# A three-stage fp32 kernel on one core: stores of a feature tile one tile later, attention loads and weight sums at other steps

## The chip, the cores and the metric

One core of a Trainium2 chip runs the whole program. The metric is the device time of one execution in microseconds (us); the times below are medians of repeated runs. The kernel is straight-line code: every engine has its own in-order list of instructions, and the order in those lists is the order in which the Python code records them. The engines are called PE (matrix multiply), DVE, ACT and POOL (element-wise work), and SP, which here only issues DMA transfers.

## The reference

Pooled attention, then two feed-forward layers, all in float32 (weights come as 64-bit floats):

```python
# attention: q, k, v are (8, 8, 576, 64); k and v are averaged over groups of 8 positions
scores = scale * q @ k_p.T
attn = softmax(scores)
x = (attn @ v_p)            # -> (4608 tokens, 512)
# first layer, w_in 512x2048, w_out 2048x512
h = x @ w_in
x = (h * clip(h + 3, 0, 6) / 6) @ w_out
# second layer, w_gate and w_val 512x1536, w_out2 1536x512
g = x @ w_gate
y = (g * sigmoid(g) * (x @ w_val)) @ w_out2
```

## The kernel before

Tokens come in nine blocks of 512 (`NB` = 9, index `j`). The program has four parts, which follow each other on PE.

**Start-up.** Attention of block 0 alone: its loads, its scores, its exponentials, until the step `block_end[0]`.

**First stage**, blocks j = 0 to 8. For each of 16 feature tiles `f` (`F1` = 16, "a slot") PE makes one tile of `h` from 12 matmuls of 128x512 (`up`, L609; two halves of a float32 split make three matmuls for each of four depth pieces). Between two such groups of 12 the attention of block j + 1 is woven in: `steps` is a list of small steps, sorted by lags from the tables `when` and `when_startup`, and `attn_slot` records the next few of it. The letters are the kinds of step: P transposes queries (DVE, L471), S makes scores (PE, L489), X takes the maximum (DVE, L499, and a subtraction at L509), A the exponential (ACT), N and M normalise (DVE, then POOL at L537), E and F split the tail (ACT, then POOL or DVE at L552), T transposes (PE, L559 and L563), U, L and V multiply with the values (PE, L587 to L590), W and Y write `x` (ACT, DVE at L602). RK and K prepare a head's keys (POOL at L390, PE at L414), R0, R1 and R a head's values (POOL at L433: `v_in` and the tail `vts`), and Q makes the low half of the values (DVE, L453 and L455); Q is the last reader of the head's `v_in` and `vts`.

After each slot's matmuls comes `gate`: DVE makes the tile `g` of the slot before (`gate1`, L625) in one of four buffers `g32`, and the tile is stored to DRAM (`store_g`, L629, 256 KB). In blocks 0 to 7 the store stands on SP's queue right behind its own gate. In block 8 it stands on ACT's queue, one gate later (`late`). ACT makes `t` from each `h` (L620). `h` has three PSUM buffers.

**Weights for the later stages.** `prep_at` gives each of 26 units ("preps": 8 of `w_out`, 12 of `w_gate`/`w_val`, 6 of `w_out2`) nine steps at slots counted from block 1 (slot 16 x (j - 1) + f): 0 loads four quarters into two `stg` buffers of three (L121, 4 x 256 KB), 1 rescales (ACT, L133), 2 and 3 join two integer halves (DVE, L139 and L142) into `q`, 4 makes four sums in `q` (POOL for the first 20 units, L205 or L210; DVE for the other six), 5 and 6 copy to `s` (ACT, L266), 7 and 8 subtract (DVE, L269), and behind 8 the unit's 1792 KB are stored from `s` (SP, L273 or L278). `q` and `s` have one buffer each.

**Second and third stage.** 63 products of the first layer's second matrix (L873) by a seven-product scheme, with the six last units made beside them, and then the second layer (L694). Their loads start in block 8: `first_loads` names loads of `gq` (L832) and `pw` (L839), 1024 KB each, at slots 0 to 9, and eight more `pw` loads follow the last tile.

**Loads of the attention** are all on SP. They are not recorded where their buffer becomes free, but a number of steps later, by the list `later`: queries (`q_in`, L374) 12 steps behind P, keys (`k_in`, L306) 8 behind RK or K, the values (`vts`, L326, and `v_in`, L319 and L320) 8 behind Q. SP takes its list in order: a transfer that waits (for a buffer, for a result to store, or for the completion of the transfer eight places ahead of it, since eight completion counters are used in turn) holds up all behind it.

Of the kernel before, what the change touches and what calls it, by code (L numbers as in the profile page):

```python
# [23 lines left out]
def kernel(  # L24
# [27 lines left out]
    nc = tc.nc  # L52
    P = 128
    B, H, S, D = q.shape
# [5 lines left out]
    F1 = w_in.shape[1] // P  # L60
    F2 = w_gate.shape[1] // P
    N = 512
    NB = NT // N
# [40 lines left out]
    NP1 = F1 // 2  # L104
    g_d = [dram.tile([P, 2, 2, NP1, MB], F32, name=f"g{j}") for j in range(NB)]
# [110 lines left out]
    prep_t = {}  # L216
    prep_at = {}
    PREP_A = 20
    for u in range(len(preps)):
        first = 11 * u // 2 if u < PREP_A else F1 * (NB - 1) + 9 * (u - PREP_A)  # L220
        for step, off in enumerate((0, 3, 4, 5, 6, 7, 8, 8, 9)):
            prep_at.setdefault(first + off, []).append((u, step))

    def prep_slot(n):
# [4 lines left out]
    def prep_step(u, step):  # L229
        kind, f, m = preps[u]  # L230
        if step == 0:
            place = A7 if kind == "up" else B7
            prep_t["q", u] = []
            for pair in ((("11", "21"), ("12", "22")) if kind == "up" else (("11", "21"), ("22", "12"))):
                t = stg_p.tile([P, WC, 2], F32, tag="stg", name="wstg")
                for i, quarter in enumerate(pair):
                    r, c = int(quarter[0]) - 1, int(quarter[1]) - 1
                    if kind == "up":
                        w = (w_gate, w_val)[m].bitcast(I32).rearrange("(k p) f -> p k f", p=P)
                        src = w[:, 2 * c:2 * c + 2, 2 * P * (2 * f + r):2 * P * (2 * f + r + 1)]  # L240
                    else:
                        row = P * (2 * f + r if kind == "dn" else NP1 * r + f)
                        w = (w_out2 if kind == "dn" else w_out).bitcast(I32)[row:row + P, :]
                        src = w[:, 4 * P * c:4 * P * (c + 1)]
                    fetch_into(t[:, WH * i:WH * (i + 1)], src)
                a, b = (place[quarter] for quarter in pair)
                prep_t["q", u].append((t, slice(a, b + 1, b - a)))
        elif step == 1:
            for s, _ in prep_t["q", u]:
                rescale(s)  # L250
        elif step in (2, 3):
            if step == 2:
                prep_t["f", u] = q7_p.tile([P, 8, WH], F32, tag="q7", name="q7")
            s, at = prep_t["q", u].pop(0)
            join(s, prep_t["f", u][:, at].bitcast(I32), 2)
        elif step == 4:
            q, eng = prep_t["f", u], nc.gpsimd if u < PREP_A else nc.vector
            if kind == "up":
                sums_a(eng, lambda n: q[:, A7[n]])
            else:  # L260
                sums_b(eng, lambda n: q[:, B7[n]])
        elif step in (5, 6):
            if step == 5:
                prep_t["s", u] = s7_p.tile([P, 7, 2, WH], F32R, tag="s7", name="s7")
            q, t, part = prep_t["f", u], prep_t["s", u], slice(0, 4) if step == 5 else slice(4, 7)
            nc.scalar.copy(out=t[:, part, 0], in_=q[:, part])  # L266
        else:
            q, t, part = prep_t["f", u], prep_t["s", u], slice(0, 4) if step == 7 else slice(4, 7)
            nc.vector.tensor_tensor(out=t[:, part, 1], in0=q[:, part], in1=f32(t[:, part, 0]), op=ALU.subtract)  # L269
            if step == 7:  # L270
                return
            if kind == "up":
                nc.sync.dma_start(  # L273
                    out=s_up[f][m].rearrange("p s a k f -> p (s a k f)"),
                    in_=f32(t).rearrange("p s a f -> p (s a f)"),
                )
            else:
                nc.sync.dma_start(out=(s_dn if kind == "dn" else s_w1)[:, :, f], in_=f32(t))  # L278
# [344 lines left out]
    def gate1(t, ps):  # L623
        g = t_p.tile([P, N], F32, tag="g32", name="g32", bufs=4)
        nc.vector.scalar_tensor_tensor(out=g, in0=t, scalar=1.0, in1=ps, op0=ALU.min, op1=ALU.mult)  # L625
        return g

    def store_g(eng, j, f, g):
        eng.dma_start(out=g_d[j][:, :, f // NP1, f % NP1], in_=g.rearrange("p (r n) -> p r n", r=2))  # L629

# [285 lines left out]
    units, unit_end, segs, heads = [], [], [], []  # L918
    seg_of, first_in_seg, first_in_head = {}, {}, {}
    for j in range(NB):  # L920
        t0 = j * N
        while t0 < (j + 1) * N:
            b, s0 = t0 // S, t0 % S
            n = min(S - s0, (j + 1) * N - t0)
# [3 lines left out]
            for p in range(KT):  # L928
# [7 lines left out]
                s = s0  # L936
                for m, qt in alone:
                    u = (b, (p,), s, m, qt)
# [5 lines left out]
                if paired and p % 2 == 1:  # L944
                    u = (b, (p - 1, p), s, paired, paired)
# [26 lines left out]
    for i in range(NU):  # L972
        startup_unit = i < unit_end[0]
        lag = dict(when_startup if startup_unit else when)
        if units[i] in early_units and not startup_unit:
            lag["A"] = lag["X"]
        stages = [(what, i) for what in "SXANMEFTULVWY"]
        if 2 <= i < 8:
            stages.append(("C", i))
        stages += [("P", n) for n in first_in_seg.get(i, ())]  # L980
        for h in first_in_head.get(i, ()):
            stages += [(what, h) for what in ("RK", "K", "R0", "R1", "R", "Q")]
        events += [(i + lag[st[0]][0], lag[st[0]][1], st[1], n, st) for n, st in enumerate(stages)]
    steps = [e[4] for e in sorted(events, key=lambda e: e[:4])]
    block_end = [1 + steps.index(("Y", e - 1)) for e in unit_end]
    for what, i in steps[:block_end[0]]:
        if what == "S":
            block_end[0] = max(block_end[0], 1 + steps.index(("X", i)), 1 + steps.index(("A", i)))

# [61 lines left out]
    def next_v(i):  # L1053
        for load, ahead in ((load_vtail, 2), (load_v, 3)):
            for h in next_heads(i, ahead):
                later.append((done[0] + 8, lambda load=load, h=h: load(*heads[h], nc.sync)))

    def do_step(st):
        what, i = st
# [51 lines left out]
    done, later = [0], []  # L1111
# [10 lines left out]
    with tc.manual_schedule():  # L1122
# [6 lines left out]
            out=vmask[:, 0], in_=vmask[:, 0], compare_op=ALU.is_ge, fill=0.0,  # L1129
# [3 lines left out]
            out=vmask[:, 1], in_=vmask[:, 1], compare_op=ALU.is_ge, fill=0.0,  # L1133
# [41 lines left out]
        gated, late = [], []  # L1175

        def gate():
            for jd, fd, t, hp in gated:
                g = gate1(t, hp)
                for args in late:  # L1180
                    store_g(nc.scalar, *args)
                late.clear()
                if jd < NB - 1:
                    store_g(nc.sync, jd, fd, g)
                else:
                    late.append((jd, fd, g))
            gated.clear()

        first_loads = dict(enumerate([
# [28 lines left out]
                        split_b(0, f - F1 + NCB)  # L1218
        gate()
        for args in late:  # L1220
            store_g(nc.scalar, *args)
        new_pw(6, big_x("pw"))
        for n in (3, 4, 5, 6):
            for h in range(2):
# [8 lines left out]
        for i in range(7 * NB):  # L1233
            j, n = divmod(i, 7)
# [85 lines left out]
```

## Time and profile before

| | us |
|---|---|
| median of 3 runs (lowest, highest) | 1828.6 (1827.26, 1830.62) |
| the profiled execution | 1828.44 |
| its span, first to last instruction | 1826.7 |
| start-up and first stage, up to the last `h` | 648.7 |
| of it the five blocks 2 to 6 | 344.7 |
| second and third stage | 1178.0 |

The span is 1.7 us shorter than the execution's time. The blocks are cut where the first matmul of each block's `h` starts on PE; blocks 2 to 6 run from 205.2 to 549.9 us.

### The profile page before, as it was taken

How to read it: one execution, taken by the hardware profiler on the slowest of the kernel's cores; microseconds unless marked ns; L12 is line 12 of the kernel's file. 1: busy time of each engine (PE TensorE's matmuls, PEld its weight loads, DVE VectorE, ACT ScalarE, POOL GpSimd, SP SyncE). 2: the span in 40 equal slices, each digit the busy share in tenths (PEclk: the TensorE clock that was granted, in tenths of full speed). 3: DMA queues.
4: the chain of work that ended last, by engine and by line, in shares of the span. 5: the costliest groups of instructions: out<-in, count | busy, mean ns of one | idle time of the engine just before them, and what ended most of it. 6: DMA issues, size and time to landing. Idle time of an engine off the chain costs nothing.

```text
span 1826.7 us, 30898 instructions
## 1 busy us (share of the span) xinstructions
PE 1725.1 (94%) x11209; PEld 1624.9 (89%) x11209; DVE 1328.9 (73%) x2356; ACT 754.7 (41%) x1657; POOL 632.9 (35%) x812
## 2 busy tenths in 40 slices
PE   5789989988989989999999899999999999999999
PEld 4668777877768789999999799999999999999999
DVE  6587778887766358878888667667678568668666
ACT  5454545544535244545554323224224224124222
POOL 6245556756542000000000153153252351361550
PEclk8799999999989999999999899999999999999999
DMA  6556878877766885455544587887887977977876
GB/s 162 136 160 181 255 237 245 283 207 244 227 191 229 332 326 197 164 191 191 179 179 162 201 289 240 296 290 235 312 277 245 321 253 252 327 248 262 282 244 216
DMA packets 235831, 432.47 MB, mean 237 GB/s; under 512 B 86688, under 2 KB 168608, under 8 KB 218528
## 3 DMA queue, kind: packets, MB, share of 16 engines
q1 hardware_dynamic: 229184, 425.00, 70.7%
q10 hardware_dynamic: 6496, 5.51, 0.9%
q8 instruction: 88, 1.44, 0.3%
q14 instruction: 63, 0.52, 0.1%
HBM read 326.11 MB, written 104.33 MB: 236 GB/s over the span
## 4 chain that ended last, share of the span: by engine, by line
PE 72%; DMA 6%; DVE 4%; POOL 1%; SPq 1%; issue 1%; ACT 1%; ACTq 0%; DVEq 0%; POOLq 0%
PE b L694 43%; PE b L873 19%; PE h L609 8%; DMA g<-g 3%; DMA q_in<-in_q_dram 1%; PE pss L489 1%; DVE g L625 1%; DMA k_in<-in_k_dram 1%; DMA vts<-in_v_dram 1%; DMA y<-o 0%; SPq L374 0%; DVE s L269 0%; PE pst L563 0%; POOL k_in L390 0%; DVE q L142 0%
## 5 line engine op out<-in xcount | busy, mean ns | idle before, releaser
L694 PE MATMUL b<-xc,wr 128*128 128x384 f32 x3024 | 527.9, 335 | 9.0 <-ACT xc L147 5.0
L694 PEld LDWEIGHTS b<-xc,wr 128*128 128x128 f32 x3024 | 525.8, 188 | 9.9 <-ACT xc L147 5.3
L609 PE MATMUL h<-x,wu 128*128 128x512 f32 x1728 | 439.2, 406 | 6.1 <-DVE g L625 6.1
L741 POOL TENSOR_TENSOR s<-s,c 128x384 f32<-128x384 f32 x144 | 142.4, 1013 | 802.8 <-ACT s L739 802.8
L703 DVE TENSOR_TENSOR c<-c,b 128x384 f32<-128x384 f32 x504 | 265.1, 552 | 178.5 <-PE b L694 154.7
L609 PEld LDWEIGHTS h<-x,wu 128*128 128x128 f32 x1728 | 326.3, 194 | 73.5 <-DVE g L625 8.0
L873 PE MATMUL b<-gb,pw 128*128 128x256 f32 x3024 | 365.7, 284 | 7.5 <-ACT gb L147 5.9
L873 PEld LDWEIGHTS b<-gb,pw 128*128 128x128 f32 x3024 | 364.4, 192 | 8.8 <-ACT gb L147 6.3
L694 PE MATMUL b<-wr,gc 128*128 128x256 f32 x2268 | 265.6, 279 | 0.0
L694 PEld LDWEIGHTS b<-wr,gc 128*128 128x128 f32 x2268 | 265.4, 188 | 0.0
L147 ACT CAST gb<-gq 128x512 fp32r<-128x512 f32 x252 | 155.4, 622 | 179.8 <-PE b L873 154.5
L148 DVE TENSOR_TENSOR gb<-gq,gb 128x512 fp32r<-128x512 f32 x252 | 167.8, 687 | 63.0 <-ACT gb L147 62.3
L748 POOL TENSOR_TENSOR gf<-s,c 128x384 f32<-128x384 f32 x144 | 168.2, 1192 | 67.0 <-DVE c L703 64.5
L147 ACT CAST gc<-gf 128x768 fp32r<-128x768 f32 x126 | 105.6, 838 | 186.9 <-POOL gf L748 100.8
L739 ACT ACTIVATE s<-c 128x384 f32<-128x384 f32 x144 | 73.4, 526 | 204.0 <-DVE c L703 202.7
L148 DVE TENSOR_TENSOR gc<-gf,gc 128x768 fp32r<-128x768 f32 x126 | 133.7, 1092 | 15.7 <-ACT gc L147 14.0
L620 ACT ACTIVATE t<-h,half 128x512 f32<-128x512 f32 x144 | 98.9, 687 | 82.9 <-PE h L609 53.4
L625 DVE SCALAR_TENSOR_TENSOR g<-t,h 128x512 f32<-128x512 f32 x144 | 97.4, 677 | 38.9 <-DMA g<-g 26.6
L711 ACT COPY c<-b 128x384 f32<-128x384 f32 x72 | 33.9, 471 | 144.5 <-PE b L694 144.5
L851 DVE TENSOR_TENSOR gq<-gq 128x1024 f32<-128x1024 f32 x72 | 87.7, 1218 | 0.0
L537 POOL TENSOR_TENSOR e<-e,sm 128x288 f32<-128x288 f32 (+4 forms) x73 | 49.0, 671 | 106.5 <-DVE sm L533 81.2
L489 PE MATMUL pss<-kbd,qT 128*128 128x144 f32 (+2 forms) x320 | 60.5, 314 | 17.0 <-DVE qT L471 12.9
(106 smaller groups left out, 1669.8 us busy)
## 6 DMA issues: line engine op xcount, KB each, us to landing
wr<-sup SPq DMA_DIRECT2D x72, 1024.0 KB
wr<-sdn SPq DMA_DIRECT2D x84, 768.0 KB
wr<-sup SPq DMA_DIRECT2D x72, 768.0 KB
gq<-g SPq DMA_DIRECT2D x36, 1024.0 KB
g<-g SPq DMA_DIRECT2D x128, 256.0 KB
sup<-s SPq DMA_DIRECT2D x12, 1792.0 KB
wstg<-in_moe_w_out_dram SPq DMA_DIRECT2D x56, 256.0 KB
sw<-s SPq DMA_DIRECT2D x8, 1792.0 KB
```

Source lines behind the costliest of these rows:

```text
L147: nc.scalar.copy(out=hi, in_=src)
L148: lo_engine.tensor_tensor(out=lo, in0=src, in1=f32(hi), op=ALU.subtract)
L489: nc.tensor.matmul(out=ps[:, i], lhsT=qT[:, :qt], rhs=kbd_t[p], start=True, stop=True)
L609: nc.tensor.matmul(out=ps, lhsT=w(kt, wh), rhs=x(kt, xh), start=first and n == 0, stop=last and n == 3 * len(kts) - 1,)
L620: nc.scalar.activation(out=t, in_=ps, func=ACTF.Relu, bias=half, scale=1.0 / 6.0)
L625: nc.vector.scalar_tensor_tensor(out=g, in0=t, scalar=1.0, in1=ps, op0=ALU.min, op1=ALU.mult)
L694: nc.tensor.matmul(out=ps, lhsT=w(wh), rhs=x(xh), start=first and n == 0, stop=last and n == 2)
L703: add = lambda dst, a, b: nc.vector.tensor_tensor(out=dst, in0=a, in1=b, op=ALU.add)
L741: nc.gpsimd.tensor_tensor(out=g[q], in0=g[q], in1=c[q], op=ALU.mult)
L748: nc.gpsimd.tensor_tensor(out=gf[p][:, GP[TURN[q]], f], in0=g[q], in1=c[q], op=ALU.mult)
L851: nc.vector.tensor_tensor(out=v(what), in0=v(a), in1=v(b), op=op)
L873: nc.tensor.matmul(out=ps[:, d], lhsT=w[:, CB * c + k, wh, P * d:P * (d + 1)], rhs=g[:, gh, k], start=what == place and (c, d, k, m) == (0 ...
```

## The change

Five edits in one. `store_g` always goes to SP, and each tile's store is recorded ahead of the next tile's gate, in all nine blocks (`late`). The values' loads come 4 steps behind Q and no longer 8. For the units of block 1, S is followed at once by X and A (lag (1, 1) for both, S being at (1, 0)), where they had (1, 13); with it the loop that moved `block_end[0]` behind the X and A of every S that falls into the start-up is gone. The weight units that POOL sums start every 6 slots and no longer every 5.5, and have ten steps: sums two slots behind the second join, and the store in a step of its own, one slot behind the last subtraction.

```diff
-        first = 11 * u // 2 if u < PREP_A else F1 * (NB - 1) + 9 * (u - PREP_A)
-        for step, off in enumerate((0, 3, 4, 5, 6, 7, 8, 8, 9)):
+        first = 6 * u if u < PREP_A else F1 * (NB - 1) + 9 * (u - PREP_A)
+        for step, off in enumerate((0, 3, 4, 5, 7, 8, 9, 9, 10, 11)):
...
-        else:
+        elif step in (7, 8):
             q, t, part = prep_t["f", u], prep_t["s", u], slice(0, 4) if step == 7 else slice(4, 7)
             nc.vector.tensor_tensor(out=t[:, part, 1], in0=q[:, part], in1=f32(t[:, part, 0]), op=ALU.subtract)
-            if step == 7:
-                return
+        else:
+            t = prep_t["s", u]
             if kind == "up":
...
-    def store_g(eng, j, f, g):
-        eng.dma_start(out=g_d[j][:, :, f // NP1, f % NP1], in_=g.rearrange("p (r n) -> p r n", r=2))
+    def store_g(j, f, g):
+        nc.sync.dma_start(out=g_d[j][:, :, f // NP1, f % NP1], in_=g.rearrange("p (r n) -> p r n", r=2))
...
         if units[i] in early_units and not startup_unit:
-            lag["A"] = lag["X"]
+            lag["X"] = lag["A"] = (1, 1)
...
-    for what, i in steps[:block_end[0]]:
-        if what == "S":
-            block_end[0] = max(block_end[0], 1 + steps.index(("X", i)), 1 + steps.index(("A", i)))
...
-                later.append((done[0] + 8, lambda load=load, h=h: load(*heads[h], nc.sync)))
+                later.append((done[0] + 4, lambda load=load, h=h: load(*heads[h], nc.sync)))
...
             for jd, fd, t, hp in gated:
-                g = gate1(t, hp)
                 for args in late:
-                    store_g(nc.scalar, *args)
-                late.clear()
-                if jd < NB - 1:
-                    store_g(nc.sync, jd, fd, g)
-                else:
-                    late.append((jd, fd, g))
+                    store_g(*args)
+                late[:] = [(jd, fd, gate1(t, hp))]
             gated.clear()
```

SP's list in block 6, from one store to the loads of the last two heads' values. Before (`g_99` is the DRAM tile of block 6, the second name the buffer that is stored; each store also waits for DVE's gate of that very tile):

```order
325 L629 DMA g_99<-g_6128 256x1x256
326 L374 DMA q_in<-in_q_dram 32x16x32 x4
327 L121 DMA wstg<-in_moe_w_gate_dram 128x2x256 x4
328 L629 DMA g_99<-g_6193 256x1x256
329 L326 DMA vts_131<-in_v_dram 16x512 x3
330 L319 DMA v_in<-in_v_dram 72x512
331 L320 DMA v_in<-in_v_dram 56x512
332 L374 DMA q_in<-in_q_dram 32x16x32 x4
333 L629 DMA g_99<-g_6264 256x1x256
334 L326 DMA vts_132<-in_v_dram 16x512 x3
```

The same place of the changed kernel, on SP:

```order
321 L629 DMA g_99<-g_6032 256x1x256
322 L374 DMA q_in<-in_q_dram 32x16x32 x4
323 L326 DMA vts_131<-in_v_dram 16x512 x3
324 L319 DMA v_in<-in_v_dram 72x512
325 L320 DMA v_in<-in_v_dram 56x512
326 L629 DMA g_99<-g_6098 256x1x256
327 L273 DMA sup_108<-s_6007 128x3584
328 L374 DMA q_in<-in_q_dram 32x16x32 x4
329 L326 DMA vts_132<-in_v_dram 16x512 x3
330 L629 DMA g_99<-g_6163 256x1x256
```

The values' loads follow the queries at once; the store that stood between them is behind them, and stores a tile whose gate is a slot old. The weight loads are elsewhere.

SP's list in the start-up, before (`q_in` of 32x2x32 are the queries of the 64 tokens with which block 1 begins):

```order
20 L374 DMA q_in<-in_q_dram 32x2x32 x8
21 L121 DMA wstg<-in_moe_w_in_dram 128x4x256 x2
22 L306 DMA k_in<-in_k_dram 72x2x512
23 L374 DMA q_in<-in_q_dram 32x2x32 x8
24 L326 DMA vts_131<-in_v_dram 16x512 x3
25 L326 DMA vts_132<-in_v_dram 16x512 x3
26 L319 DMA v_in<-in_v_dram 72x512
27 L320 DMA v_in<-in_v_dram 56x512
```

And of the changed kernel, on SP at the same place:

```order
22 L306 DMA k_in<-in_k_dram 72x2x512
23 L326 DMA vts_131<-in_v_dram 16x512 x3
24 L326 DMA vts_132<-in_v_dram 16x512 x3
25 L319 DMA v_in<-in_v_dram 72x512
26 L320 DMA v_in<-in_v_dram 56x512
27 L319 DMA v_in<-in_v_dram 72x512
28 L320 DMA v_in<-in_v_dram 56x512
29 L319 DMA v_in<-in_v_dram 72x512
30 L320 DMA v_in<-in_v_dram 56x512
31 L374 DMA q_in<-in_q_dram 32x2x32 x8
```

The second eight query loads have moved behind twelve loads of values.

SP's list at the start of block 8 (`g_100` and `g_101` are the DRAM tiles of blocks 7 and 8). Before, where the stores of block 8 are on ACT's list:

```order
364 L629 DMA g_100<-g_7063 256x1x256
365 L832 DMA gq<-g_93 128x2048
366 L273 DMA sup_114<-s_7039 128x3584
367 L839 DMA pw<-sw_102 128x2048 x2
368 L832 DMA gq<-g_93 128x2048
369 L839 DMA pw<-sw_102 128x2048 x2
370 L832 DMA gq<-g_93 128x2048 x2
371 L839 DMA pw<-sw_102 128x2048 x10
```

The changed kernel, on SP:

```order
363 L273 DMA sup_112<-s_6980 128x3584
364 L839 DMA pw<-sw_102 128x2048
365 L629 DMA g_101<-g_7051 256x1x256
366 L121 DMA wstg<-in_moe_w_val_dram 128x2x256 x4
367 L839 DMA pw<-sw_102 128x2048
368 L629 DMA g_101<-g_7073 256x1x256
369 L832 DMA gq<-g_93 128x2048
370 L629 DMA g_101<-g_7098 256x1x256
371 L839 DMA pw<-sw_102 128x2048
372 L629 DMA g_101<-g_7123 256x1x256
```

The stores alternate with the large loads, and weight units 17 to 19 are not yet done: `sup_112`, and later `sup_113` and `sup_114`, are stored in block 8, where before it was `sup_114` alone, and one unit's four loads fall there too.

## Rows read from the trace of the kernel before

**Rows 1.** Windows by stage: stretch: length, busy PE, PEld, DVE, ACT, POOL (instructions), clock, DMA share, GB/s.

```profile
67.10:147.00 79.90, 71.17 (x402) 59.13 (x401) 59.98 (x133) 46.24 (x167) 38.16 (x62) 0.93 0.59 159
205.20:549.90 344.70, 308.00 (x1572) 255.82 (x1571) 266.02 (x623) 172.39 (x464) 210.76 (x326) 0.95 0.78 238
549.90:602.30 52.40, 52.40 (x265) 44.23 (x264) 35.71 (x76) 27.80 (x61) 12.60 (x20) 1.00 0.63 230
602.30:648.70 46.40, 44.42 (x194) 35.91 (x193) 14.35 (x20) 14.20 (x21) 0.00 (x0) 1.00 0.96 355
648.70:660.60 11.90, 6.59 (x50) 5.89 (x48) 3.80 (x6) 2.54 (x5) 0.00 (x0) 0.89 0.94 356
660.60:1020.00 359.40, 357.25 (x2962) 356.66 (x2963) 298.29 (x423) 180.36 (x297) 0.00 (x0) 0.99 0.53 186
1020.00:1826.70 806.70, 793.44 (x5307) 792.35 (x5306) 564.92 (x877) 249.57 (x422) 310.55 (x288) 0.99 0.79 269
```

**Rows 2.** Waits of the engines: us in total, times, longest us.

```profile
PE pst L563 <- POOL et L552: 30.0, 11, 8.4
POOL q L205 <- DVE q L142: 25.0, 6, 13.5
POOL vts L433 <- DMA vts<-in_v_dram: 24.1, 7, 8.4
```

**Rows 3.** Waits of SP's own queue, same columns, first row of the store's line.

```profile
SPq L629 <- DVE g L625: 48.2, 23, 9.7
```

**Rows 4.** Timeline of all engines around PE's longest stall: start, us, instruction [idle before <- what ended it].

```profile
509.22 0.52 SPq L629 DMA_DIRECT2D g<-g  x1
...
515.96 0.71 DVE L471 STREAM_TRANSPOSE qT<-q_in 128x512 f32<-128x512 f32 x1 [2.12 <-DMA q_in<-in_q_dram]
...
517.19 0.73 DVE L455 SCALAR_TENSOR_TENSOR vtl<-vts,vtl 32x64 fp32r<-32x64 f32 x1
...
519.34 0.52 SPq L629 DMA_DIRECT2D g<-g  x1
...
519.95 1.48 SPq L326 DMA_DIRECT2D vts<-in_v_dram  x3
...
524.97 1.64 POOL L433 TENSOR_TENSOR vts<-vts 96x256 f32<-96x256 f32 x3 [7.13 <-DMA vts<-in_v_dram]
...
528.98 0.34 PE L563 MATMUL pst<-ident,et 64*96 64x64 f32 x1 [8.36 <-POOL et L552]
```

**Rows 5.** Chain that ended last: twelve `h` matmuls behind two stalls, and undisturbed.

```profile
274.49 4.53 PE h L609 x12
...
529.31 5.42 PE h L609 x12
...
535.81 2.81 PE h L609 x12
```

**Rows 6.** Waits of the engines for stores of a tile.

```profile
DVE g L625 <- DMA g<-g: 26.6, 6, 5.8
...
ACT gb L147 <- DMA g<-g: 9.2, 1, 9.2
```

**Rows 7.** Timeline of all engines, start-up.

```profile
43.79 2.74 SPq L326 DMA_DIRECT2D vts<-in_v_dram  x6
...
45.23 0.24 DVE L471 STREAM_TRANSPOSE qT<-q_in 128x64 f32<-128x64 f32 x1 [0.61 <-DMA q_in<-in_q_dram]
...
45.82 0.69 DVE L142 SCALAR_TENSOR_TENSOR gb<-wstg,gb 128x512 int32<-128x512 int32 x1
...
49.55 6.53 SPq L374 DMA_DIRECT2D q_in<-in_q_dram  x8
...
57.96 1.33 PE L489 MATMUL pss<-kbd,qT 128*128 128x144 f32 x4 [6.63 <-DVE qT L471]
```

**Rows 8.** The page's DMA issues: how often, KB each.

```profile
sup<-s SPq DMA_DIRECT2D x12, 1792.0 KB
...
wstg<-in_moe_w_val_dram SPq DMA_DIRECT2D x24, 256.0 KB
```

More of the change, by code (lines that the diff above doesn't have):

```diff
@@ L1220 @@
         for args in late:
-            store_g(nc.scalar, *args)
+            store_g(*args)
         new_pw(6, big_x("pw"))
```

## The prediction

> **What bounds the kernel now.** I read the windows by stage first, because a change in one stage is worth what PE loses there, and not its share of the whole [rows 1]. The reader is to see two kinds of stretch. From 660.6 us to the end PE stands still for 359.40 - 357.25 = 2.2 us and 806.70 - 793.44 = 13.3 us: these stages are bound by PE's own matmuls, and since their PE list is the same in both kernels, I count nothing there. Blocks 2 to 6 are another matter: 344.70 us, of which PE works 308.00, so 36.7 us are stalls, at a mean granted clock of 0.95; and block 0 stalls for 79.90 - 71.17 = 8.7 us. Block 7 shows what a block is like without them: 52.40 us, no stall, clock 1.00.
>
> Next I ask what PE waits for there. The list of waits names the tail of the softmax: PE's transposes wait 30.0 us for POOL's `et` (L552), and POOL, just ahead of that instruction in its list, waits 24.1 us for the values' tails from DRAM and 25.0 us for DVE's joined weights [rows 2]. Then the timeline of the longest such stall, 8.36 us, read backwards [rows 4]: PE at 528.98 waits for POOL; POOL had waited 7.13 us, until 524.97, for a load of `vts` that SP issued only at 519.95. The buffer of that load was free when DVE's L455 (the step Q) ended, at 517.19 + 0.73 = 517.92. In between stood a store that waited for its own gate and was issued at 519.34. SP's own waits show that this is common: the store's line waits 48.2 us for the gate alone, 23 times, with further DVE instructions near it in rows behind [rows 3]. So the fault is one of order: SP holds loads back behind a result that is not there yet. After a stall PE also works at the lower of its two clock levels for a while: the 12 matmuls that take 2.81 us undisturbed take 4.53 us behind the first and 5.42 us behind the last of five stalls in blocks 2 to 6 [rows 5].
>
> **The change part by part**, against the profiled 1828.4 us (span 1826.7 and 1.7 around it; the median of the runs is 0.2 higher).
>
> *Blocks 1 to 6: stores one tile behind their gate, values 4 steps earlier, weight sums and weight stores a slot later.* A store now finds its gate done a slot ago, so SP's wait on it goes, and the 128 stores still cost the same 0.52 us of issue each. For the stall of 8.36 us: the load can follow Q directly, which is worth 519.95 - 517.92 = 2.0 us. Ahead of it in the same chain DVE sat 2.12 us waiting for queries, and their load too was issued behind a store, at 509.22; that wait can go as well. Together 4.1 of 8.36 us, one half. I found no second thing in the other stalls of this kind that would make them better or worse in proportion, so I take one half of all 36.7 us, 18 us. The wait of POOL for the joins (25.0 us) belongs to the same pool of stalls, since it delays the same `et`, and the sums that now stand a slot later remove it at the source; I don't add it a second time. The slow matmuls behind the five stalls cost some 10 us (1.7 and 2.6 us more behind the first and the last, 2 on the mean, five times); half of it, 5. **-23 us.** Bounds: nothing at all, if what comes next in the chain is as late (then SP waits for the landing of data instead), and -47, if all stalls go (36.7 + 10). A g32 buffer is held one slot longer: in blocks 0 to 7 DVE never waited for a store to land, all 26.6 us of that wait being in block 8 [rows 6], and four buffers with slots of some 4.3 us (344.70 / 80) leave three slots for a store, so I count zero; if it didn't fit, each miss would show as the 4 to 6 us that it takes in block 8.
>
> *Block 0: X and A straight behind S.* A score tile is given back to PE's ring of two as soon as ACT has made the exponentials, so key transposes that wait for it start earlier. The price is that DVE and ACT stand in order behind a score that PE has not made yet, ahead of `gate` and of L620. Of the 8.7 us I take a third, **-3 us**; bounds +3 and -8.
>
> *Start-up.* The values' loads, due 4 steps earlier, now stand ahead of the second eight query loads. Six of them take SP 2.74 us and the other six about as much, so the queries are issued some 5 us later, and DVE, which takes its list in order, makes their transposes not at 45.23 but at about 50.4 [rows 7]. Behind these stands the join that frees a weight buffer: it ended at 45.82 + 0.69 = 46.5 and will end at about 51.7. SP's next weight load waits for it, and behind that load stand the eight queries that were issued from 49.55 on and that the score waited for at 57.96, with PE idle for 6.63 us. SP came to them 49.55 - 46.5 = 3.0 us behind the join, part of it with the values' loads, so they slip by 5.2 less what of these 3.0 falls away: between 2 and 5 us. **+3 us**, bounds 0 (the transfers land sooner on a free queue) and +5. That `block_end[0]` is earlier moves one key transposition behind the first 12 matmuls; PE does both in either order, so nothing.
>
> *Block 8.* Two things. Six slots per unit instead of five and a half bring two more weight stores of 1792 KB and four weight loads of 256 KB into the block: 4.7 MB [rows 8], at the 355 GB/s of this stretch 13 us of transfers, in the only stretch of the first stage where the DMA engines are full (0.96 and 0.94 of their time) [rows 1]. And the 16 stores leave ACT's queue and stand between the large loads on SP. The Trainium skill speaks against that: Perfetto Trace Analysis, in its section DMA Optimizations, would give inputs and outputs to different issuing engines; by it alone this term would be the 13 us of its upper bound. In favour: ACT, whose first casts for the second stage stood 9.2 us behind its own stores [rows 6], is free, and PE's 11.90 - 6.59 = 5.3 us between the last `h` and the steady second stage fall into that wait. Transfers of slots 0 to 9 (10 loads of 1024 KB, the stores, three weight units) are more than ten slots of 2.8 us can carry, but slots 10 to 15 ask for little, so half of the 13 us should be caught up, and I count half of the 5.3 as gained: 6.7 - 2.7, **+4 us**, bounds -5 and +13.
>
> *Second and third stage.* The last six units get their later steps too, sums on DVE a slot later, the store a slot behind. PE never waited for them here; zero, with the same 15.5 us of stalls left as they are.
>
> Sum: 1828.4 + 3 - 3 - 23 + 4 = 1809.4, by the median 1809.6 us.
>
> **The rivals.** *Everything goes* (0.08): if the late issue is the only cause, all of blocks 2 to 6 is gained and most of block 0: -47 - 6 + 3 + 0, 1778 us. Against it: POOL's chain behind a landed `vts` is itself 4 us long (524.97 to 528.98), and DVE works 266.02 of 344.70 us, so it would be at 0.89 of the time if 47 us went.
>
> *The wait moves* (0.15): SP runs ahead of DVE, and stands a little later at the next thing, the Q step that the values' loads now wait for themselves, or the landing of the transfer eight places ahead. What the stores no longer wait, the loads do; the DMA engines are at 0.78 in these blocks, and `q_in` is issued in small pieces. Then -7 there, 0 in block 0, and the +3 and +4 stay: 1828.6 us, no change.
>
> *Block 8 decides* (0.16), on the other side: a store behind up to seven transfers of 1 MB on one queue lands after 7.3 MB / 355 GB/s, 20 us; DVE has four tile buffers and PE three of `h`, together some 10 us of slots, so gate, and with it PE, run at the pace of the transfers, and the whole 13 us fall on the path. With the start-up's 3 that is +16, and it decides where blocks 0 to 6 give back less than 16 us; with half of my gain there (-11) the time is 1833 us. The rule of the Trainium skill just cited would send it this way. For it speaks that the DMA share is 0.96 already, against it that PE lost just 46.40 - 44.42 = 2.0 us inside the block while stores took their time on ACT's queue.
>
> **How the numbers follow.** My forecast, one half of the stalls, has 0.61, and its own range is 1794 to 1824 (a quarter to three quarters of the blocks' 47, with the other terms at the sum). A measurement of this kernel tells a change from none at about 0.2%, 3.7 us. Faster: all of the forecast and of *everything goes*, and a fifth of *the wait moves*: 0.72. The same: 0.09, most of *the wait moves*. Slower: *block 8 decides* and a fifth of *the wait moves*, 0.19. For eight times in ten the range reaches from 1788, which leaves out *everything goes*, to 1834, which takes in both other rivals; the corner of all bad bounds (5 + 3 + 0 + 13, 1849) is left out.
>
> **What would show it.** In the profile after: SP's waits on the store's line fall from dozens of us to a few; loads of `vts` follow L455 within 1 us; POOL's waits for `vts` and for joins halve; the five stalls of PE in blocks 2 to 6 are shorter and the stretch takes about 320 us; the score at 57.96 comes at about 61; block 8 takes about 4 us longer up to the steady second stage. It is wrong if POOL still waits as long for `vts` though they were issued early, if DVE's gate waits for stores in blocks 0 to 7, or if block 8 lasts 10 us longer than 46.4.

## The result and the profile after

The changed kernel takes 1798.75 us (median of 4 runs, 1796.84 to 1801.43), the kernel before on the same chip 1829.3: a ratio of 0.9835, 95% interval 0.9818 to 0.9852, some 30 us less. The profiled execution took 1801.43 us, its span is 1799.6.

The windows by stage of the changed kernel, with the columns of [rows 1] and cut at the same places of the program (the first `h` matmul of a block; the last three rows divide the second and third stage elsewhere):

```profile
64.30:144.70 80.40, 72.40 (x433) 59.97 (x433) 62.94 (x136) 46.66 (x164) 41.81 (x67) 0.95 0.65 173
201.90:521.10 319.20, 302.56 (x1572) 251.11 (x1571) 267.17 (x614) 168.93 (x461) 205.47 (x318) 0.98 0.78 238
521.10:573.50 52.40, 52.40 (x265) 44.20 (x264) 33.83 (x74) 26.36 (x58) 12.67 (x20) 1.00 0.67 233
573.50:627.30 53.80, 48.01 (x195) 37.51 (x194) 22.63 (x33) 18.85 (x28) 5.74 (x8) 0.94 1.02 397
627.30:660.00 32.70, 29.59 (x243) 29.19 (x243) 20.23 (x28) 15.24 (x26) 0.00 (x0) 0.99 0.89 351
660.00:1000.00 340.00, 335.77 (x2789) 335.07 (x2787) 286.89 (x407) 171.72 (x281) 0.00 (x0) 1.00 0.52 183
1000.00:1799.60 799.60, 790.98 (x5286) 790.37 (x5286) 559.96 (x872) 246.07 (x417) 310.81 (x288) 0.99 0.79 268
```

25.5 of the 27.1 us by which the span is shorter are in blocks 2 to 6: 319.20 us where there were 344.70. PE does the same 1572 matmuls there; it is idle for 319.20 - 302.56 = 16.6 us instead of 36.7, and its busy time falls from 308.00 to 302.56 us, at a mean granted clock of 0.98 instead of 0.95. Block 8 is the one that got longer: 53.80 us instead of 46.40, its clock 0.94 instead of 1.00, idle 5.8 us instead of 2.0.

The waits of the engines in blocks 2 to 6 (201.9 to 521.1 us), which answer to [rows 2]:

```profile
PE pst L563 <- POOL et L552: 11.7, 4, 5.3
DVE qT L471 <- DMA q_in<-in_q_dram: 7.6, 6, 3.2
POOL vts L433 <- DMA vts<-in_v_dram: 7.3, 2, 5.2
POOL q L205 <- DVE q L142: 1.7, 1, 1.7
```

The same four rows of the kernel before, in its blocks 2 to 6 (205.2 to 549.9 us):

```profile
PE pst L563 <- POOL et L552: 28.8, 8, 8.4
POOL vts L433 <- DMA vts<-in_v_dram: 23.8, 6, 8.4
DVE qT L471 <- DMA q_in<-in_q_dram: 16.6, 6, 6.8
POOL q L205 <- DVE q L142: 9.6, 4, 4.7
```

All four fell: the transposes wait less for the softmax's tail, and what stood ahead of it in the chain (the queries, the values' tails, the joined weights) is late less often. The place of the stall of [rows 4], 8.36 us (the 143rd of 160 `et` transposes on PE in each kernel), reads in the timeline of the changed kernel:

```profile
490.46 3.92 SPq L326 DMA_DIRECT2D vts<-in_v_dram  x3
...
492.44 0.71 DVE L471 STREAM_TRANSPOSE qT<-q_in 128x512 f32<-128x512 f32 x1
...
496.44 2.00 POOL L433 TENSOR_TENSOR vts<-vts 96x256 f32<-96x256 f32 x3
...
501.25 0.26 PE L563 MATMUL pst<-ident,et 64*96 64x64 f32 x1 [1.65 <-POOL et L552]
```

The queries cost DVE no wait, POOL takes the values' tails without one, and PE stands still for 1.65 us.

### The profile page after: what moved, and what is told of

The parts are those of the page before. It is cut to its first block, busy times and chain, and to the rows that moved or that the text cites. A ratio compares the mean times of both kernels' runs of the same rounds, so it can differ in the third digit from the quotient of the medians.

```text
span 1799.6 us, 30919 instructions
## 1 busy us (share of the span) xinstructions
PE 1717.7 (95%) x11209; PEld 1618.0 (90%) x11209; DVE 1336.2 (74%) x2356; ACT 754.4 (42%) x1657; POOL 634.7 (35%) x812
## 4 chain that ended last, share of the span: by engine, by line
PE 69%; DMA 8%; DVE 4%; issue 1%; SPq 1%; ACT 1%; POOL 1%; ACTq 0%; DVEq 0%; POOLq 0%
PE b L694 44%; PE b L873 17%; PE h L609 7%; DMA pw<-sw 1%; DMA wstg<-in_moe_w_out_dram 1%; DMA g<-g 1%; DVE g L625 1%; DMA gq<-g 1%; DMA wstg<-in_moe_w_val_dram 1%; DVE s L269 1%; DMA y<-o 1%; DMA q_in<-in_q_dram 0%; PE pss L489 0%; SPq L374 0%; DMA vts<-in_v_dram 0%
## 5 line engine op out<-in xcount | busy, mean ns | idle before, releaser
L873 PE MATMUL b<-gb,pw 128*128 128x256 f32 x3024 | 364.2, 283 | 3.4 <-ACT gb L147 2.8
L873 PEld LDWEIGHTS b<-gb,pw 128*128 128x128 f32 x3024 | 363.6, 192 | 4.1 <-ACT gb L147 3.0
L625 DVE SCALAR_TENSOR_TENSOR g<-t,h 128x512 f32<-128x512 f32 x144 | 97.5, 677 | 33.5 <-DMA g<-g 23.5
L537 POOL TENSOR_TENSOR e<-e,sm 128x288 f32<-128x288 f32 (+4 forms) x73 | 47.4, 649 | 110.1 <-DVE sm L533 85.5
```

Of the source, the lines that this page charges most:

```text
L873: nc.tensor.matmul(out=ps[:, d], lhsT=w[:, CB * c + k, wh, P * d:P * (d + 1)], rhs=g[:, gh, k], start=what == place and (c, d, k, m) == (0 ...
```

## The experiments

The sum of the prediction laid the gain to the stores and the values' loads together. Against this stand two other readings: that another of the four parts makes it (weight units, start-up), or that no part does by itself, since what SP no longer waits for at one entry of its list it waits for at the next. Eight kernels take one part each, or all but one. All lengths in this table are in us, cut as above; the last column runs from the first `h` of block 8 to the end of the span. Ratios are to the kernel before on the same chip, with 95% intervals.

| kernel | median | ratio | start-up | block 0 | block 1 | blocks 2-6 | block 8 | from block 8 on |
|---|---|---|---|---|---|---|---|---|
| before | 1829.3 | 1 | 67.2 | 79.8 | 58.2 | 344.7 | 46.5 | 1224.4 |
| after | 1798.75 | 0.9835 (0.9818, 0.9852) | 64.3 | 80.4 | 57.2 | 319.2 | 53.7 | 1226.1 |
| stores_alone | 1824.28 | 0.9965 (0.9949, 0.9981) | 68.5 | 80.2 | 58.7 | 343.9 | 50.4 | 1223.8 |
| values_alone | 1831.72 | 1.0004 (0.9992, 1.0015) | 70.8 | 79.3 | 61.0 | 341.8 | 47.7 | 1226.7 |
| weights_alone | 1831.74 | 1.0009 (0.9997, 1.0021) | 66.7 | 79.1 | 57.2 | 345.9 | 54.5 | 1227.3 |
| early_alone | 1828.97 | 0.9983 (0.9970, 0.9996) | 61.8 | 83.8 | 58.7 | 345.9 | 47.4 | 1224.3 |
| after_old_stores | 1826.23 | 0.9977 (0.9965, 0.9988) | 63.7 | 81.1 | 57.2 | 342.7 | 55.0 | 1227.9 |
| after_old_values | 1799.25 | 0.9833 (0.9811, 0.9855) | 62.4 | 79.5 | 57.2 | 318.9 | 53.2 | 1225.8 |
| after_old_weights | 1813.93 | 0.9913 (0.9893, 0.9932) | 63.4 | 79.7 | 58.6 | 338.9 | 46.2 | 1222.7 |
| after_old_early | 1803.49 | 0.9847 (0.9827, 0.9867) | 69.0 | 79.2 | 57.2 | 318.1 | 53.3 | 1225.9 |

Block 7 takes 52.4 or 52.5 us in all of them. Kernels with the same start-up list differ there by about 1 us (63.2 to 64.3 over seven kernels), so less than that is not read. The lengths are those of one profiled execution: that of `stores_alone` took 1829.48 us, the longest of its eleven runs and 5.2 above the median, that of `after_old_weights` 1817.71, 3.8 above it, that of the changed kernel 2.7 above it.

**One part on the kernel before.** `stores_alone` stores one tile behind the gate, with block 8 still on ACT's queue:

```diff
                 for args in late:
-                    store_g(nc.scalar, *args)
+                    store_g(nc.scalar if args[0] == NB - 1 else nc.sync, *args)
...
+                late[:] = [(jd, fd, gate1(t, hp))]
```

> The kernel before, with the stores of blocks 0 to 7 one tile behind their gate on SP; block 8 keeps its stores on ACT, the rest is as before. If the order of SP's queue made the gain (the theory), this is the larger half of it: 10 to 16 us faster (1813 to 1819), blocks 2 to 6 some 12 us shorter than 344.7. If the weight units made it, or the place of the values' loads alone, it is within 4 us of the kernel before.

`values_alone` has the loads 4 steps behind Q:

```diff
-                later.append((done[0] + 8, lambda load=load, h=h: load(*heads[h], nc.sync)))
+                later.append((done[0] + 4, lambda load=load, h=h: load(*heads[h], nc.sync)))
```

> The kernel before, with the loads of the values 4 steps behind Q. Theory: 4 to 8 us faster (1821 to 1825), since the loads still stand behind stores that wait for their own gate. If the place of these loads alone made the gain: 15 to 25 us faster (1804 to 1814). If the weight units made it: no change.

`weights_alone` has the ten steps and the 6 slots (the change's first two pieces):

```diff
-        first = 11 * u // 2 if u < PREP_A else F1 * (NB - 1) + 9 * (u - PREP_A)
-        for step, off in enumerate((0, 3, 4, 5, 6, 7, 8, 8, 9)):
+        first = 6 * u if u < PREP_A else F1 * (NB - 1) + 9 * (u - PREP_A)
+        for step, off in enumerate((0, 3, 4, 5, 7, 8, 9, 9, 10, 11)):
...
```

> The kernel before, with weight units every 6 slots, ten steps, sums two slots behind the join and the store in a step of its own. Theory: 2 to 6 us faster in blocks 2 to 6, of which block 8 takes some back: within 4 us of the kernel before. If the weight units made the gain: 15 to 25 us faster (1804 to 1814).

`early_alone` has X and A straight behind S, and no loop that moves the end of the start-up:

```diff
-            lag["A"] = lag["X"]
+            lag["X"] = lag["A"] = (1, 1)
...
-    for what, i in steps[:block_end[0]]:
-        if what == "S":
-            block_end[0] = max(block_end[0], 1 + steps.index(("X", i)), 1 + steps.index(("A", i)))
```

> The kernel before, with X and A straight behind S for the units of block 1, and the start-up ending with its own last step. Theory: 1 to 5 us faster (1824 to 1828), from the stall of 2.59 us ahead of the first tile and the stalls of block 0; blocks 2 to 6 unchanged at 344 us. A rival by which the values' loads, and not this edit, made the start-up shorter has no change here.

No part alone gives more than 0.35%, and blocks 2 to 6 stay between 341.8 and 345.9 us in all four. The theory missed twice: `stores_alone` gained 6 us by the medians and not 10 to 16, `values_alone` nothing and not 4 to 8. `weights_alone` stayed within 4 us as it said, but gained nothing in blocks 2 to 6 where it said 2 to 6; `early_alone` is 1.5 us faster, inside its 1 to 5. The parts don't add: 0.35% and 0.17% are gained by the stores and by the start-up's edit, nothing by the other two, against 1.65% by all of them.

**All parts but one.** Each takes one of these pieces back from the changed kernel (in `after_old_stores` the stores of block 8 are again on ACT's queue).

> The changed kernel with the stores as before (blocks 0 to 7: on SP right behind their own gate; block 8: on ACT). No part alone shortened blocks 2 to 6 by more than 3 us, the change does by 25, so parts must need each other. Theory now: several things hold each late load back one after the other (store, distance from Q, weight units ahead of it), and each alone only uncovers the next; then taking any one out loses most: here 1812 to 1822, blocks 2 to 6 at 332 to 342. Rival, two parts make it (values and weights, say) and the stores are idle: 1797 to 1804, blocks 2 to 6 at about 320.

> The changed kernel with the values' loads 8 steps behind Q as before. Theory of several covers: loses most, 1812 to 1822. If stores and weight units are the pair that makes it: 1797 to 1804. POOL's wait for vts in blocks 2 to 6 (7 us after, 24 before) tells it beside the time.

> The changed kernel with the weight units as before (every 5.5 slots, nine steps). Theory of several covers: loses most, 1812 to 1822, although block 8 has less to move (its part is 7 us shorter). If stores and values are the pair: 1792 to 1802.

> The changed kernel with X and A of block 1's units at (1, 13) and the start-up that ends behind them, as before. They touch only the start-up and block 0, so by either theory 2 to 5 us are lost (1801 to 1804), all of it before 150 us, and blocks 2 to 6 stay at about 320. If the place at which the start-up ends decides what stands where in the later blocks: more than 8 us are lost, in blocks 2 to 6.

Two parts turn out to be necessary: without the late stores blocks 2 to 6 take 342.7 us, without the new weight units 338.9 (what `after_old_weights` keeps of the gain, 11 us of the span, is 5.8 us in these blocks, 3.9 in start-up and block 0, 1.7 from block 8 on). The values' 4 steps change nothing (318.9 us, total as after). The start-up's edit gives up to 4.7 us of the total by the medians, with overlapping intervals, and by the lengths 3.5 us in start-up and block 0. So the theory of several covers, by which any part taken out loses most, is wrong for the values' loads, and `after_old_stores` lost more than it said (1826.23 us for 1812 to 1822); the rival that stores and values are the pair is wrong by `after_old_weights`. Stores and weight units alone, without both other parts, were not run.

Why the stores alone bring little is seen in the waits of SP's own queue in blocks 2 to 6. Before:

```profile
SPq L629 <- DVE g L625: 31.1, 13, 9.7
SPq L629 <- DVE x L602: 17.4, 15, 2.7
...
SPq L273 <- DVE s L269: 6.1, 6, 2.5
...
SPq L278 <- DVE s L269: 4.0, 4, 2.9
```

`stores_alone`:

```profile
SPq L273 <- DVE s L269: 36.4, 7, 9.9
SPq L278 <- DVE s L269: 8.6, 6, 3.1
...
SPq L629 <- DVE g L625: 3.8, 8, 1.2
```

`after_old_weights`:

```profile
SPq L273 <- DVE s L269: 35.7, 8, 9.5
SPq L278 <- DVE s L269: 5.9, 3, 3.2
...
SPq L629 <- DVE g L625: 2.8, 7, 0.6
```

The changed kernel:

```profile
SPq L629 <- DVE aT L579: 19.2, 13, 3.9
SPq L629 <- DVE sm L531: 8.2, 6, 2.7
...
SPq L273 <- DVE s L269: 3.8, 3, 2.4
SPq L629 <- DVE g L625: 3.6, 5, 1.8
...
SPq L278 <- DVE s L269: 2.7, 2, 2.4
```

With late stores and the old weight units the wait for the gate is gone (31.1 us to 3.8 and 2.8), and a wait of the same size stands at the weight unit's store, which follows its own last subtraction: 6.1 + 4.0 us before, 36.4 + 8.6 in `stores_alone`, 35.7 + 5.9 in `after_old_weights`. With late stores and the new weight units, neither is there. The other way round, with the new weight units and the old stores, it is the store's line that waits: all its rows in blocks 2 to 6 sum to 81.3 us before, 97.5 in `weights_alone`, 93.6 in `after_old_stores` and 56.4 in the changed kernel. The stall of [rows 4] shows the same in the timeline of `after_old_weights`:

```profile
490.29 0.52 SPq L629 DMA_DIRECT2D g<-g  x1
...
498.28 0.94 DVE L269 TENSOR_TENSOR s<-q,s 128x768 fp32r<-128x768 f32 x1
...
499.29 0.35 SPq L273 DMA_DIRECT2D sup<-s  x1
...
500.26 4.89 SPq L374 DMA_DIRECT2D q_in<-in_q_dram  x4
...
508.25 0.71 DVE L471 STREAM_TRANSPOSE qT<-q_in 128x512 f32<-128x512 f32 x1 [2.20 <-DMA q_in<-in_q_dram]
...
510.61 1.33 SPq L326 DMA_DIRECT2D vts<-in_v_dram  x3
...
516.05 1.64 POOL L433 TENSOR_TENSOR vts<-vts 96x256 f32<-96x256 f32 x3 [5.99 <-DMA vts<-in_v_dram]
...
520.05 0.34 PE L563 MATMUL pst<-ident,et 64*96 64x64 f32 x1 [7.36 <-POOL et L552]
```

SP issues nothing from 490.81 to 499.29, until the subtraction that ends at 498.28 + 0.94 = 499.22; a store and a lot of queries follow, whose four issues take 4.89 us and for which DVE waits; behind them SP has another store, another lot of queries and four weight loads; the values' tails are issued at 510.61, POOL waits 5.99 us, and PE 7.36.

**Which piece of the weight units.** Two kernels divide them: `units_55` keeps the weight store in its own step and takes the rest back, `store_at_sub` keeps the 6 slots alone.

```diff
--- units_55, against the changed kernel
-        first = 6 * u if u < PREP_A else F1 * (NB - 1) + 9 * (u - PREP_A)
-        for step, off in enumerate((0, 3, 4, 5, 7, 8, 9, 9, 10, 11)):
+        first = 11 * u // 2 if u < PREP_A else F1 * (NB - 1) + 9 * (u - PREP_A)
+        for step, off in enumerate((0, 3, 4, 5, 6, 7, 8, 8, 9, 10)):
--- store_at_sub, against the changed kernel (the store again behind step 8)
-        for step, off in enumerate((0, 3, 4, 5, 7, 8, 9, 9, 10, 11)):
+        for step, off in enumerate((0, 3, 4, 5, 6, 7, 8, 8, 9)):
```

> The changed kernel, with its weight units again 11u/2 slots apart and the sums one slot behind the second join, but with the weight store still in a step of its own, one slot behind the last subtraction. Theory A (the store of a weight unit must not stand directly behind its own subtraction in SP's list; the spacing matters little): blocks 2 to 6 take 319 to 325 us as in the changed kernel, total about 1799 to 1804. Theory B (what matters is the spacing, 6 slots in place of 5.5, through the load that waits for its buffer): blocks 2 to 6 take 335 to 340 us as with the whole old schedule (338.9), total about 1814. Theory C (both by parts): about 328 us, total about 1806.

> The changed kernel, with the nine old steps of a weight unit (sums one slot behind the second join, the weight store directly behind the last subtraction), but the units still 6 slots apart. Theory A (the separate weight store is what the feature stores need beside them): blocks 2 to 6 take 335 to 340 us, total about 1814. Theory B (the spacing is): 319 to 325 us, total about 1799 to 1804. Theory C (both by parts): about 328 us, total about 1806.

**Block 8.** `after_act8` puts the stores of block 8 on ACT's queue, still one tile behind their gate:

```diff
                 for args in late:
-                    store_g(*args)
+                    store_g(nc.scalar if args[0] == NB - 1 else nc.sync, *args)
...
```

> The changed kernel, with the feature stores of block 8 alone issued by ScalarE, one tile behind their gate as the others. Theory A (the 7 us that block 8 got longer come from its stores on SP, which hold the loads behind them in SP's list): block 8 takes 47 to 49 us in place of 53.7, and total falls to 1792 to 1796. Theory B (they come from the weight units, whose steps are later in block 8; weights alone gave 54.5 us and the old weight steps 46.2): block 8 stays at 52 to 55 us and the total within 0.2% of 1799.

| kernel | median | ratio | start-up | block 0 | block 1 | blocks 2-6 | block 8 | from block 8 on |
|---|---|---|---|---|---|---|---|---|
| units_55 | 1800.11 | 0.9830 (0.9813, 0.9846) | 63.2 | 79.1 | 57.2 | 326.9 | 45.2 | 1219.2 |
| store_at_sub | 1809.81 | 0.9888 (0.9873, 0.9903) | 63.4 | 79.6 | 58.5 | 322.9 | 53.0 | 1230.8 |
| after_act8 | 1800.62 | 0.9837 (0.9823, 0.9852) | 63.8 | 79.1 | 57.2 | 318.5 | 54.9 | 1227.1 |
| units_mixed | 1787.54 | 0.9765 (0.9752, 0.9778) | 63.9 | 79.2 | 57.2 | 316.2 | 46.0 | 1220.2 |

In `units_55` blocks 2 to 6 take 12 us less than with the whole old schedule, by the weight store's own step alone, 326.9 us; in `store_at_sub` the 6 slots alone take off 16 (322.9). Both by parts, then, in these blocks. The weight store still stands behind its own subtraction in `store_at_sub`, and SP waits less for it there, though still long (24.1 us, where `after_old_weights` has 41.6):

```profile
SPq L273 <- DVE s L269: 16.0, 5, 5.4
...
SPq L278 <- DVE s L269: 8.1, 3, 3.7
```

So that wait is one of the things that hold blocks 2 to 6 back, and not the only one; what else the 6 slots do stays open. In the total the weight store's step is worth all (1800.11, as after) and the 6 slots a quarter (1809.81 between 1813.93 and 1798.75), for the 6 slots cost block 8 some 7 us: it takes 53 to 55 us in every kernel that has them throughout, and 45 to 50 in the others. The queue of block 8's stores isn't the cause: on ACT's it takes 54.9 us (theory B of `after_act8`).

The timeline of block 8 of the changed kernel, which begins at 573.5 us, has the weight stores that SP issues there, three where the kernel before has one, and a gate that waits 6.68 us for an earlier tile's store to land, with PE behind it:

```profile
576.21 0.34 SPq L273 DMA_DIRECT2D sup<-s  x1
...
598.25 0.32 SPq L273 DMA_DIRECT2D sup<-s  x1
...
615.63 0.69 DVE L625 SCALAR_TENSOR_TENSOR g<-t,h 128x512 f32<-128x512 f32 x1 [6.68 <-DMA g<-g]
...
616.38 1.22 PE L609 MATMUL h<-x,wu 128*128 128x512 f32 x2 [4.34 <-DVE g L625]
...
620.36 0.83 SPq L273 DMA_DIRECT2D sup<-s  x1
```

**A version without that cost.** `units_mixed` has the weight store in its own step, ten units 6 slots apart and ten 5, so that the twentieth is done with early in block 8:

```diff
-        first = 6 * u if u < PREP_A else F1 * (NB - 1) + 9 * (u - PREP_A)
-        for step, off in enumerate((0, 3, 4, 5, 7, 8, 9, 9, 10, 11)):
+        first = 6 * u - max(u - 10, 0) if u < PREP_A else F1 * (NB - 1) + 9 * (u - PREP_A)
+        for step, off in enumerate((0, 3, 4, 5, 6, 7, 8, 8, 9, 10)):
```

> The changed kernel with the sums again one slot behind the second join and the weight store one slot behind the last subtraction, its first ten weight units 6 slots apart and the next ten 5, so that the twentieth starts at slot 105 and is done with by slot 115 (at 6 slots: 114 to 125, in block 8, whose slots are 112 to 127). Theory A (the long block 8 comes from weight units that run into it, and the gain of blocks 2 to 6 from the separate weight store, helped by the 6 slots): blocks 2 to 6 take 319 to 323 us, block 8 about 46 us in place of 53.7, the span falls by 5 to 8 us, to about 1792 to 1795. Theory B (work and loads of the weight units cost the same wherever they stand): what block 8 gives, blocks 5 and 6 take, as with 11u/2 slots (45.2 us in block 8, 326.9 in blocks 2 to 6), and the total stays at 1798 to 1801.

It takes 1787.54 us by the median, 11 less than the changed kernel; the intervals of the two ratios, 0.9752 to 0.9778 and 0.9818 to 0.9852, lie apart. Its span of 1789.1 us is 10.5 shorter: 5.9 from block 8 on, 3.0 in blocks 2 to 6, 1.6 ahead of them. Its windows of blocks 2 to 6 and of block 8:

```profile
200.30:516.50 316.20, 301.95 (x1572) 251.83 (x1571) 266.69 (x620) 171.06 (x464) 206.47 (x322) 0.97 0.83 249
569.00:615.00 46.00, 45.45 (x195) 35.74 (x194) 15.40 (x22) 14.22 (x21) 2.87 (x4) 1.00 0.98 380
```

Both come together, and by more than was expected of theory A: 316.20 us although the second ten units stand closer, and block 8 with 0.55 us of stalls, at a clock of 1.00. One weight store is left in block 8, and it is issued early in it:

```profile
577.02 0.33 SPq L273 DMA_DIRECT2D sup<-s  x1
```

Moved out of block 8, where the DMA share is 0.98 to 1.02, into blocks where it is 0.83, the same work no longer shows in the time. Whether its transfers or its work on the engines costs block 8 the 7 us was not separated.

## Why the prediction was right, and where its steps were not

The time, 1798.75 us, is 11 us below the forecast and inside its range, and faster was the likeliest sign. Step by step:

- **Blocks 1 to 6**, forecast -23: measured 58.2 + 344.7 to 57.2 + 319.2, -26.5. The size came out by the reckoning: one half of the stalls, 18 us, measured 36.7 - 16.6 = 20.1; the clock 5, measured 308.00 - 302.56 = 5.4. The mechanism was only part of it, and the fit of the size is in part luck: stores and values' loads, to which the prediction gave the gain, bring 5.8 us of the 25 in blocks 2 to 6 while the weight units stay as before (`after_old_weights`). The later weight store stood in the heading of that term and got no price. The runs show that stores and weight units are both needed: with one of them left as before, all but 1 to 6 us of the 25 are kept back (343.9, 342.7 and 338.9 us). On the side of the stores it is the store behind its own gate; on the side of the weight units it is in part the weight store behind its own subtraction (`units_55`) and in part the spacing (`store_at_sub`).
- **The joins**, counted in the same pool: the 25.0 us of [rows 2] are of the whole span, of which 9.6 lie in blocks 2 to 6, and 1.7 are left. That the later sums do it is not shown: `units_mixed`, with its sums one slot behind the join as before, has 1.5 us there.
- **"The load can follow Q directly, which is worth 2.0 us"** did not happen so. With 8 steps instead of 4 the blocks take 318.9 us, the same. At the stall of [rows 4] the queries and the values' tails are early because SP is earlier altogether. The step also gave the store too much: SP was issuing four weight loads (L121) until 518.76 us there, so that of the 2.0 us the store can have cost 519.95 - 518.76 = 1.2.
- ***The wait moves***, held at 0.15, is what the stores do by themselves: `stores_alone` has 343.9 us in these blocks. Only the place was wrong: not the Q step, not a landing, but in the main the weight unit's store of a fresh result.
- **"SP's waits on the store's line fall from dozens of us to a few"** is wrong. Over the whole span the row of [rows 3] goes from 48.2 only to 44.9 us, and in blocks 2 to 6 the gate's own row falls to 3.6 while others of DVE at the same line grow (`aT` from 7.4 to 19.2, `sm` from 6.5 to 8.2). SP's queue as a whole waits 109.6 us in these blocks before and 100.1 after, though they are 25 us shorter. What told the difference was the consumers' side, 23.8 us to 7.3 for `vts`: SP's waits hold up less of what is needed next. Why the waits at the store's line end with instructions near the gate, and not with the gate, stays open.
- **Block 0**, forecast -3, and **start-up**, +3, must be read together, since the end of the start-up moved: the start-up measured -2.9 and block 0 +0.6, together -2.3 where the sum was 0. The step on the queries came true almost to the number, as the timeline of the changed kernel shows:

```profile
47.71 3.65 SPq L374 DMA_DIRECT2D q_in<-in_q_dram  x8
50.97 0.24 DVE L471 STREAM_TRANSPOSE qT<-q_in 128x64 f32<-128x64 f32 x1 [9.04 <-DMA q_in<-in_q_dram]
...
53.40 0.69 DVE L142 SCALAR_TENSOR_TENSOR gb<-wstg,gb 128x512 int32<-128x512 int32 x1
...
54.65 4.43 SPq L374 DMA_DIRECT2D q_in<-in_q_dram  x8
...
60.79 1.33 PE L489 MATMUL pss<-kbd,qT 128*128 128x144 f32 x4 [3.90 <-DVE qT L471]
...
64.26 1.05 PE L609 MATMUL h<-x,wu 128*128 128x512 f32 x2
```

  The transposes stand at 50.97 (said: 50.4) instead of 45.23, the score at 60.79 (said: about 61) instead of 57.96 [rows 7], and `values_alone` has a start-up of 70.8 us, +3.6. What failed is "so nothing" for the earlier `block_end[0]`: the first `h` comes 64.26 - 60.79 = 3.5 us behind that score, where it was 67.16 - 57.96 = 9.2. `early_alone` measures it apart: start-up -5.4, and block 0 +4.0 instead of -3, since, by my reading, the work that the first `h` no longer waits for is done behind it. The edit is worth -1.4 us there over both stretches, and -3.5 in the changed kernel (from 148.2 in `after_old_early` to 144.7).
- **Block 8 and handover**, forecast +4: 46.5 us of block 8 and 36.7 from the last `h` to the start of the 241st matmul of L873 before, 53.7 and 31.5 after, +2.0. In the changed kernel a last stall of 2.77 us ends just there, and by the 401st matmul, behind the slow ones that follow it, the difference is +4.1. The first term, +6.7 for the weight units that come into block 8, measured 53.7 - 46.5, +7.2, and `units_mixed`, `units_55` and `weights_alone` show that this is its cause. The second, -2.7 because the stores leave ACT's queue, is not borne out: the handover did shorten by 5.2 us, but it also did with the stores on ACT's queue and the new weight units (32.8 us in `weights_alone`, 33.3 in `after_old_stores`, 32.4 in `after_act8`). Against `after_act8` the changed kernel gains 1.0 us from block 8 on, and the totals, 1798.75 and 1800.62, don't tell them apart.
- ***Block 8 decides***, held at 0.16, fell: block 8 got longer by the 7.2 us of the weight units and not by its stores on SP, and it did not outweigh the gain ahead of it. DVE did wait for stores to land in the changed kernel's block 8, 23.5 us in all, about as before (26.6 [rows 6]), and nowhere in blocks 0 to 7. The rule of the Trainium skill (Perfetto Trace Analysis, DMA Optimizations), by which it may make sense to give inputs and outputs to different issuing engines, made no difference that can be measured here: `after_act8`, which follows it for the stores of block 8, has a ratio of 0.9837, the changed kernel, which does not, 0.9835.
- **Second and third stage**, 0: from the 241st matmul of L873 to the end 1141.2 us before, 1140.9 after, and from the 401st 1122.1 and 1119.8. `store_at_sub` and `after_old_weights` take 1144.9 from the 241st, and 1122.5 and 1123.6 from the 401st; why is left open.
- **The range** of the forecast alone, a quarter to three quarters of 47 us with the other terms at the sum, works out at 1797 to 1821 and not 1794 to 1824. The result lies inside either, near the lower end.

## What to carry to other kernels

On a queue that issues in order, look for every entry that waits for a result just made. Here two kinds of stores did, and with the feature stores, or the weight units together with their store, left as they were the gain in blocks 2 to 6 was 1 to 6 of 25 us, so that each edit alone looked useless. What helped both was a slot between producer and store; for the second kind another spacing of the units helped as much. Measure such a queue by its consumers' waits for the data, not by how long the queue itself waits (109.6 us here before, 100.1 after). And when steps are spread over time, see where the last of them land: the same weight units cost nothing that shows in blocks with a DMA share of 0.8, and 7 us in the one with 1.0.

## What the runs showed of the hardware

The clock, in these rows a mean over its two levels of 1.2 and 2.4 GHz, took its share both ways with the same matmuls on PE. Blocks 2 to 6 rose from 0.95 to 0.98 when the stalls shortened. Block 8 fell from 1.00 to 0.94: PE stood still for 4.34 us until 616.38, and the stretch around it is the one at a lower clock.

```profile
614.00:622.00 8.00, 5.62 (x14) 4.45 (x15) 4.06 (x6) 2.21 (x5) 0.00 (x0) 0.57 1.01 394
622.00:627.30 5.30, 5.30 (x26) 4.36 (x25) 3.19 (x5) 2.22 (x4) 0.00 (x0) 1.00 0.98 392
```

The 195 matmuls of the changed kernel's window took 48.01 us of busy time, against 44.42 us for 194 before and 45.45 us for 195 in `units_mixed`, both at 1.00. The prediction counted the gain in blocks 2 to 6 and not this loss: of the 7.4 us that block 8 lost by the windows, 3.6 are PE's busy time and 3.8 its idle time.
